# Scores behind each attend in a shared PSUM ring, fp32 scores for the first twelve pairs, and a planner that knows the shared port

## The chip, the cores and the metric

The kernel runs on one core of one Trainium2 chip. Its engines work side by side and meet through semaphores: PE (TensorE, matmuls; PEld is its weight load), ACT (ScalarE), DVE (VectorE), POOL (GpSimd), and SP, which issues all DMAs. SBUF holds tiles; PSUM, 8 banks of 2 KB for each of 128 partitions, takes what PE computes. The metric is the device time of one execution in microseconds, the median of several runs.

## The reference

Attention with a sigmoid in place of a softmax, then a gated product with a short convolution:

```python
scores = scale * np.matmul(q, k.transpose(0, 1, 3, 2)) - np.log(S)   # (8, 12, 448, 64)
attn = 1.0 / (1.0 + np.exp(-scores))
x = np.matmul(attn, v)                       # heads joined: (8, 448, 768)
gate_pre = sum over k of conv_w[k] * xp[:, k:k+S, :]     # 5 taps over time, per channel
gate = 1.0 / (1.0 + np.exp(-gate_pre))
out = (gate * (x @ w_val)) @ w_out
```

All inputs and the output are fp32.

## The kernel before

Two heads make a pair (128 channels on the partitions), so there are 8 x 6 = 48 pairs; six pairs are one batch. The first 12 pairs (FIRST_PAIRS) are batches 0 and 1; for them there are no products to run beside, or few.

**Precision.** Most matmuls work on values split into a high part in fp32r and a low remainder, three passes for one product (high x high, low x high, high x low). `split_qk` (L346) makes qk_hi by a cast on DVE or ACT and qk_lo by a subtraction on POOL (`sub`, L293), two of each for every pair. `scores` (L360, matmuls at L374) then multiplies keys and queries in three passes; the two heads use the two halves of the array's rows (64*128 tiles) at once. The keys beyond 3 x 128 of both heads form a fourth chunk, which uses all rows (`scores_rest`, L380, matmuls at L386).

**Attention.** `attention` (L390) applies the sigmoid on ACT. For the first 12 pairs it writes fp32 (a_single), and `attend` (L436) multiplies it with v in plain fp32. From pair 12 on the sigmoid stays in PSUM (L398), a scaled fp16 copy (L410, ACT) and its remainder (L411, DVE) go to the tile `a`, and v is scaled by a power of two and split into two fp16 parts as well (`v_scale`, L414). That power comes from the largest |v| (L443), spread over the partitions by a one-column matmul with ones at the end of an attend two pairs earlier (L464) into a spare column of ps_x, and worked out by one step on DVE (L421) and three on POOL (L423, L425, L427). In `attend`, L455 is the fourth chunk with all rows and columns, L461 the others, two heads in the two column halves (128*64 tiles).

**Gate and products.** `after` (L468) copies ps_x to x (L282 or L288), splits it into xs, and builds the gate from x by five taps (L290 or L288, then four of L508) and a sigmoid (L510). Batch 0 goes to a scratch in DRAM, and a seventh of it is loaded back behind each later batch's rows (L484, L501), so that a product has 448 + 64 = 512 columns. `product` (L515, matmuls at L529) is one block of 128 output channels: six parts of three matmuls, `val` from xs, then, gated at L541, `out` from g. There are 12 such products for each of seven batches.

**Weights.** `weight` (L320) loads 24 blocks as 64-bit words and turns each into fp32 on DVE (L313, L315, L329) and ACT (L317), then splits it (ACT and POOL).

**PSUM.** Before the change: two score tiles of two banks (ps_sc), one bank for the fourth chunk (ps_c3), one for attend's result (ps_x), two for products (ps_m).

**Order.** Nothing is in order of the source. Each step is put on record by `op` with the engines that may run it and their cost (`ways`), a due time (`prio`), and what it reads and writes. `tau(i)` is the due time of pair i: FIRST = 7.0 us a pair for the first 12, STEP after. `Plan.issue` (L137) then runs through time: each engine that is free takes the ready step with the smallest due time, and the steps are emitted in that order. A ring's tile may be taken again when all who used its last content are done. On the chip each engine's queue then runs strictly in this order. In the plan before, scores are groups of one chunk (first 12 pairs) or of two chunks (L580) with due times of their own, spread over a pair's time.

Of the kernel before, what the change touches and what calls it, by code (L numbers as in the profile page):

```python
# [23 lines left out]
P = 128  # L24
# [63 lines left out]
class Op:  # L88
    __slots__ = ("ways", "prio", "emit", "deps", "n", "start", "end", "eng", "after", "size")

    def __init__(self, n, ways, prio, emit, size):
        self.n, self.ways, self.prio, self.emit, self.size = n, ways, prio, emit, size
        self.deps, self.after = set(), None
        self.start = self.end = self.eng = None


class Plan:
# [39 lines left out]
    def issue(self):  # L137
# [12 lines left out]
        events, order, bus = [], [], 0.0  # L150
# [48 lines left out]
def attention_then_gate(  # L199
# [42 lines left out]
    a_ring = ring(sb, 5, [P, 2, 2 * S], F16, "a")  # L242
# [53 lines left out]
    FIRST, STEP = 7.0, 13.7  # L296
# [7 lines left out]
    def at_share(i, c):  # L304
        return ((0, 0.2, 0.5, 0.6) if i < FIRST_PAIRS else (0, 1 / 3, 2 / 3, 0.9))[c]


    def convert(w, t, prio, wide):
# [4 lines left out]
        op({"V": 0.6 * c}, prio, lambda e: nc.vector.tensor_scalar(  # L313
            low(), low().bitcast(U32), 2.0**-29, 7.0, op0=ALU.mult, op1=ALU.min), [], [t])
        op({"V": 0.8 * c}, prio + 0.1, lambda e: nc.vector.scalar_tensor_tensor(  # L315
            low(), high(), -0x80000000, low(), op0=ALU.bitwise_and, op1=ALU.bitwise_or), [], [t])
        op({"A": 0.55 * c}, prio + 0.2, lambda e: nc.scalar.activation(  # L317
            high().bitcast(F32), high().bitcast(F32), AF.Copy, scale=REBIAS), [], [t])

    def weight(n, j):  # L320
# [8 lines left out]
        op({"V": 0.7}, prio + 0.3, lambda e: nc.vector.scalar_tensor_tensor(  # L329
# [3 lines left out]
        op({"A": 0.51}, prio + 0.4, lambda e: copy(e, part(h), single().bitcast(F32)), [t], [h])  # L333
        op({"G": 1.2}, prio + 0.5, lambda e: sub(
# [11 lines left out]
    def split_qk(i):  # L346
# [3 lines left out]
        for n, cs in enumerate((slice(0, S), slice(S, QW))):  # L350
            op({"V": 0.4, "A": 0.58}, t - 11 + n, lambda e, cs=cs: copy(e, h()[:, cs], x()[:, cs]), [x], [h])
        for n, cs in enumerate((slice(0, S), slice(S, QW))):
            op({"G": 1.4}, t - 9 + n, lambda e, cs=cs: sub(
                e, l()[:, cs], x()[:, cs], h()[:, cs].bitcast(F32)), [x, h], [l])

    def terms(s):
        h, l = s["h"], s["l"]
        return (h, h), (l, h), (h, l)

    def scores(group):  # L360


        bufs, reads = [], []
        for i, c in group:
            b = st[i]["ps", c] = ps_sc.new()
            bufs.append(b)
            reads += [st[i]["h"], st[i]["l"]]

        def emit(e):
            for (i, c), b in zip(group, bufs):  # L370
                for n, (k, q) in enumerate(terms(st[i])):
                    for h, rows in enumerate(halves):
                        at = S + c * P
                        mm(b()[:, h, :S], k()[rows, at : at + P], q()[rows, :S],  # L374
                           start=(n == 0), stop=(n == 2))

        i, c = group[-1]
        op({"P": 0.4 + 0.585 * len(group)}, tau(i) + share(i, at_share(i, c)), emit, reads, bufs)

    def scores_rest(i):  # L380
        s = st[i]
        b = s["ps", 3] = ps_c3.new()

        def emit(e):
            for n, (k, q) in enumerate(terms(s)):
                mm(b()[:, :S], k()[:, QW - P :], q()[:, :S], start=(n == 0), stop=(n == 2))  # L386

        op({"P": 0.61}, tau(i) + share(i, at_share(i, 3)), emit, [s["h"], s["l"]], [b])

    def attention(i, c):  # L390

        s, t = st[i], tau(i) + share(i, at_share(i, c))
        b = s["ps", c]
        cost = 0.92 if c < 3 else 0.55
        p = (lambda: b()[:, :, :S]) if c < 3 else (lambda: b()[:, :S])
# [11 lines left out]
        a = s["a", c] = a_ring.new()
        part = lambda n: a()[:, :, n * S : (n + 1) * S] if c < 3 else a()[:, 0, n * S : (n + 1) * S]
        op({"A": cost}, t + 1, lambda e: sigmoid(p()), [], [b])
        op({"A": cost}, t + 2, lambda e: nc.scalar.activation(part(0), p(), AF.Copy, scale=A_SCALE), [b], [a])  # L410
# [240 lines left out]
```

## Time and profile before

| what | us |
|---|---|
| median of 3 runs | 674.22 |
| lowest, highest run | 672.52, 676.32 |
| the profiled execution | 673.52 |
| its span, first to last instruction | 671.7 |

A profile is one execution. Its page gives the busy time of each engine, the span in 40 slices, the chain of work that ended last, and the costliest groups of instructions; the trace behind it answers questions by window, tile or line. The ends of matmuls are modelled: the pace of PE is read from the starts. A row of the timeline has its start, its length, the engine, the line, what is written from what, the tile (rows*columns of the array for PE), and how many instructions are merged; in brackets stands idle time before it and what ended it. A row of a tile's view has the shortest, median and longest duration in ns; a row of waits has the total, the number of times and the longest.

### The profile page before, as it was taken

The page shows a single profiled execution, that of the slowest core. Times are in us where ns is not written, and L with a number is a line of the kernel's source. Part 1 is how long each engine was busy: PE and PEld are TensorE (multiplying, and loading weights), DVE is VectorE, ACT ScalarE, POOL GpSimd, SP SyncE. Part 2 cuts the span into 40 slices and gives each one's busy share as a digit, 9 for nine tenths or more (in the row PEclk, how much of TensorE's full clock was granted, in tenths as well). Part 3 has the DMA queues.
Part 4 walks back from the last instruction along what each step waited for, and adds up shares of the span by engine and source line. Part 5 has one row for each costly group of instructions (what it writes and reads, how often), then busy time and mean ns, then how long its engine had stood idle before and what let it go on. Part 6 is the DMA issues. An engine that isn't in the chain of part 4 may idle for free.

```text
span 671.7 us, 9920 instructions
## 1 busy us (share of the span) xinstructions
PE 645.9 (96%) x3540; PEld 441.7 (66%) x3540; DVE 511.3 (76%) x708; ACT 437.6 (65%) x671; POOL 311.0 (46%) x313
## 2 busy tenths in 40 slices
PE   7888889899999999999999999999999999999997
PEld 5433344577767777677776777767777677776786
DVE  4999999889759897598975989759897598864410
ACT  6777756667766677666776667766677666774111
POOL 4888766645334453344533445334453344520100
PEclk9899989799999999999999999999999999999999
DMA  7889542312333123321234212332123411011001
GB/s 284 273 278 299 171 149 60 111 51 70 102 96 85 52 70 102 109 71 52 71 101 116 65 52 70 101 110 72 52 71 102 121 58 52 25 49 44 1 33 62
DMA packets 49537, 65.66 MB, mean 98 GB/s; under 512 B 26448, under 2 KB 34128, under 8 KB 49488
## 3 DMA queue, kind: packets, MB, share of 16 engines
q1 hardware_dynamic: 49488, 65.03, 32.0%
q8 instruction: 28, 0.46, 0.3%
q14 instruction: 21, 0.17, 0.1%
HBM read 49.86 MB, written 15.15 MB: 97 GB/s over the span
## 4 chain that ended last, share of the span: by engine, by line
PE 81%; DVE 10%; DMA 3%; issue 3%; ACT 2%; POOL 1%; SPq 0%; DVEq 0%; POOLq 0%; ACTq 0%
PE ps_m L529 53%; PE ps_sc L374 11%; PE ps_x L461 10%; PE ps_x L455 3%; PE ps_c L386 3%; DVE gate L508 3%; DVE w_words L329 2%; DVE w_words L315 1%; DMA w_words<-w_val 1%; DVE w_words L313 1%; DMA first_x<-x 1%; DVE gate L290 1%; DVE qk_hi L284 1%; ACT a_single L398 1%; DMA xs<-first_xs 1%
## 5 line engine op out<-in xcount | busy, mean ns | idle before, releaser
L508 DVE SCALAR_TENSOR_TENSOR gate<-x,cw,gate 128x515 f32<-128x515 f32 (+3 forms) x168 | 167.6, 997 | 2.3
L529 PE MATMUL ps_m<-xs,w_val_hi 128*128 128x512 f32 x504 | 164.3, 407 | 3.1 <-DMA xs<-first_xs 2.6
L293 POOL TENSOR_TENSOR qk_lo<-qk_src,qk_hi 128x448 fp32r<-128x448 f32 x96 | 138.0, 1445 | 58.7 <-DVE qk_hi L284 29.4
L529 PE MATMUL ps_m<-g,w_out_hi 128*128 128x512 f32 x504 | 160.9, 400 | 0.0
L411 DVE SCALAR_TENSOR_TENSOR a<-ps_sc,a 128x896 f16<-128x896 f32 x108 | 115.0, 1078 | 1.2 <-ACT a L410 1.1
L529 PEld LDWEIGHTS ps_m<-xs,w_val_hi 128*128 128x128 f32 x504 | 92.8, 191 | 29.7 <-issue 6.9
L529 PEld LDWEIGHTS ps_m<-g,w_out_hi 128*128 128x128 f32 x504 | 92.4, 188 | 25.1 <-issue 4.0
L398 ACT ACTIVATE ps_sc<-ps_sc 128x896 f32<-128x896 f32 x108 | 93.1, 898 | 22.1 <-PE ps_sc L374 22.1
L529 PE MATMUL ps_m<-xs,w_val_lo 128*128 128x512 f32 x252 | 100.8, 400 | 0.0
L529 PE MATMUL ps_m<-g,w_out_lo 128*128 128x512 f32 x252 | 99.9, 397 | 0.0
L410 ACT ACTIVATE a<-ps_sc 128x896 f16<-128x896 f32 x108 | 96.7, 921 | 0.0
L293 POOL TENSOR_TENSOR xs<-x,xs 128x448 fp32r<-128x448 f32 x48 | 68.8, 1433 | 55.1 <-DVE xs L284 36.5
L374 PE MATMUL ps_sc<-qk_hi 64*128 64x448 f32 x288 | 62.9, 434 | 15.3 <-ACT a_single L398 14.5
L421 DVE TENSOR_SCALAR v_exp<-ps_x 128x1 int32<-128x1 int32 x36 | 5.7, 158 | 87.0 <-PE ps_x L464 55.5
L423 POOL TENSOR_SCALAR v_exp<-v_exp 128x1 int32<-128x1 int32 x36 | 10.6, 294 | 127.6 <-DVE v_exp L421 127.5
L293 POOL TENSOR_TENSOR g<-y,g 128x512 fp32r<-128x512 f32 x27 | 35.4, 1310 | 68.2 <-ACT g L282 58.5
L461 PE MATMUL ps_x<-a,v_hi 128*64 128x448 f16 x432 | 59.7, 357 | 0.0
L374 PEld LDWEIGHTS ps_sc<-qk_hi 64*128 64x128 f32 x288 | 27.2, 186 | 49.2 <-ACT a_single L398 20.4
L288 ACT ACTIVATE x<-ps_x,v_exp 128x448 f32<-128x448 f32 x36 | 23.0, 638 | 51.9 <-PE ps_x L464 40.6
L529 PEld LDWEIGHTS ps_m<-xs,w_val_lo 128*128 128x128 f32 x252 | 47.9, 190 | 11.7
L529 PEld LDWEIGHTS ps_m<-g,w_out_lo 128*128 128x128 f32 x252 | 47.3, 188 | 11.5
L374 PE MATMUL ps_sc<-qk_hi,qk_lo 64*128 64x448 f32 x288 | 53.2, 366 | 0.8 <-POOL qk_lo L293 0.8
(69 smaller groups left out, 959.3 us busy)
## 6 DMA issues: line engine op xcount, KB each, us to landing
qk_src<-qk SPq DMA_DIRECT2D x48, 480.0 KB, 3.6
v_src<-vs SPq DMA_DIRECT2D x48, 256.0 KB, 2.7
out_t<-y SPq DMA_DIRECT2D x42, 224.0 KB, 2.0
w_words<-w_val SPq DMA_DIRECT2D x12, 384.0 KB, 4.0
w_words<-w_out SPq DMA_DIRECT2D x12, 384.0 KB, 3.5
first_xs<-xs SPq DMA_DIRECT2D x6, 448.0 KB, 4.1
xs<-first_xs SPq DMA_DIRECT2D x42, 64.0 KB, 3.2
x<-first_x SPq DMA_DIRECT2D x42, 34.0 KB, 1.8
```

Of the source, the lines that this page charges most:

```text
L288: nc.scalar.activation(to, x, AF.Copy, scale=by)
L293: engines[eng].tensor_tensor(to, x, y, op=ALU.subtract)
L329: op({"V": 0.7}, prio + 0.3, lambda e: nc.vector.scalar_tensor_tensor(single(), single(), 3, t()[:, :, 0], op0=ALU.logical_shift_left, op1 ...
L374: mm(b()[:, h, :S], k()[rows, at : at + P], q()[rows, :S], start=(n == 0), stop=(n == 2))
L386: mm(b()[:, :S], k()[:, QW - P :], q()[:, :S], start=(n == 0), stop=(n == 2))
L398: nc.scalar.activation(to, p(), AF.Sigmoid, bias=-math.log(S), scale=1.0 / math.sqrt(D))
L410: op({"A": cost}, t + 2, lambda e: nc.scalar.activation(part(0), p(), AF.Copy, scale=A_SCALE), [b], [a])
L411: op({"V": 1.09 if c < 3 else 0.62}, t + 3, lambda e: nc.vector.scalar_tensor_tensor(part(1), p(), A_SCALE, part(0), op0=ALU.mult, op1=ALU ...
L455: mm(px()[:, :S], v()[:, :P], x(3)[:, 0, at : at + S], start=(n == 0), stop=False, skip_group_check=True)
L461: mm(px()[rows, :S], v()[:, o : o + D], x(c)[:, h, at : at + S], start=False, stop=(c == 2 and n == len(parts) - 1), skip_group_check=True)
L508: op({"V": 0.85}, t + 1 + j, lambda e, j=j: nc.vector.scalar_tensor_tensor(g()[:, j:], x()[:, : T + HALO - j], w(j), g()[:, j:], op0=ALU.m ...
L529: mm(po(), w()[:, c, :], x()[:, k, :], start=(c == 0 and j == 0), stop=(c == NC - 1 and j == 2))
```

## The change

- **Scores of the first 12 pairs in fp32.** They are not split any more: `terms` gives a single pass on the loaded qk tile itself.
- **One PSUM ring.** ps_sc, ps_c3 and ps_x become `ps_a`, three tiles of two banks, used in the order in which they are asked for. From pair 12 on that is: fourth chunk of pair i + 1, attend's result of pair i, chunks 0, 1, 2 of pair i + 1.
- **A chain on PE.** `attend` is two steps (the one-column matmul, the fourth chunk and chunks 0 and 1; then chunk 2), followed by the scores of the next pair (of the pair after the next among the first 12), chunks 0 and 1, then 2. Through the new field `then`, PE takes nothing else in between; the first step of an attend also waits until the sources of those scores are there.
- **The planner's port.** A step marked with port may run on DVE or POOL only while no other such step holds their shared port; YIELD lets a step with an earlier due time go first. Steps that read PSUM have port="". Costs are set anew, and more steps may run on either of two engines.
- **Other moves.** The steps that read PSUM get much earlier due times (t - 20, t - 30); the three steps for the power of two move from POOL to DVE; the load of first_xs moves from t + 2 to t - 6; tiles: a 5 to 3 and a_rest 2, g (and the weight words with it) 4 to 3, g2 2 to 3; STEP 13.7 to 13.6.

```diff
@@ Plan.issue
+                for _, n in ready[e]:
+                    o = self.ops[n]
+                    if held[e] not in (None, o):
+                        continue
+                    if e not in "VG" or e not in o.port:
+                        break
+                    x = "G" if e == "V" else "V"
+                    sooner = any(p < o.prio and x in self.ops[k].port for p, k in ready[x][:4])
+                    if port <= t and not (sooner and free[x] < t + self.YIELD):
+                        break
+                else:
                     continue
-                o = self.ops[heapq.heappop(q)[1]]
-                done.add(o.n)
+                for x in o.ways:
+                    ready[x].remove((o.prio, o.n))
+                held[e] = o.then
...
+                if e in "VG" and e in o.port:
+                    port = t + cost
@@ tiles
-    a_ring = ring(sb, 5, [P, 2, 2 * S], F16, "a")
+    a_ring = ring(sb, 3, [P, 2, 2 * S], F16, "a")
+    rest_ring = ring(sb, 2, [P, 1, 2 * S], F16, "a_rest")
...
-    g_ring = ring(sb, 4, [P, 2, T], F32R, "g")
-    g2_ring = ring(sb, 2, [P, 2, T], F32R, "g2")
+    g_ring = ring(sb, 3, [P, 2, T], F32R, "g")
+    g2_ring = ring(sb, 3, [P, 2, T], F32R, "g2")
...
-    ps_sc = ring(ps, 2, [P, 2, 512], F32, "ps_sc")
-    ps_c3 = ring(ps, 1, [P, 512], F32, "ps_c3")
-    ps_x = ring(ps, 1, [P, 512], F32, "ps_x")
+    ps_a = ring(ps, 3, [P, 2, 512], F32, "ps_a")
@@ scores
+    def terms(i):
+        if i < FIRST_PAIRS:
+            return ((st[i]["qk"],) * 2,)
+        h, l = st[i]["h"], st[i]["l"]
         return (h, h), (l, h), (h, l)
...
+        return op({"P": cost}, tau(i) + 0.1 * cs[0], emit, sources(i), bufs)
@@ v_scale
-        op({"G": 0.4}, t + 0.2, lambda _: nc.gpsimd.tensor_scalar(
+        op({"V": 0.12}, t + 0.2, lambda _: nc.vector.tensor_scalar(
...
@@ attend
+        first = op({"P": 2.5 if single else 2.0}, t, lambda e: (rest(e), chunks((0, 1))),
+                   [a[0], a[1], a[3], *values] + ([ones, m] if m else []), [px])
+        first.then = op({"P": 0.76 if single else 0.56}, t, lambda e: chunks((2,)), [a[2], *values], [px])
+        return first
@@ after
-            out_of_ps = {"A": 0.64}, t, lambda e: scaled(e, own(), px()[:, :S], v()[:, 3:4].bitcast(F32)), [px, v]
+            out_of_ps = {"A": 0.64}, t - 20, lambda e: scaled(e, own(), px()[:, 0, :S], v()[:, 3:4].bitcast(F32)), [px, v]
...
+        if f:
+            op({"S": 0.1}, t - 6, lambda e: nc.sync.dma_start(
+                xs()[:, :, S:].bitcast(F32), first_xs[c]()[:, :, n : n + SL]), [first_xs[c]], [xs], P * 1024)
@@ the main order
+    for i in range(FIRST_PAIRS, NPAIRS):
+        split_qk(i)
+
+    def score(i, after=None):
+        first = scores(i, (0, 1))
+        first.then = scores(i, (2,))
+        if after:
+            after.then.then = first
+            after.deps.update(d for b in sources(i) for d in b.writers)
+        for c in range(3):
+            attention(i, c)
+
+    def rest(i):
+        scores_rest(i)
+        attention(i, 3)
+
+    for i in range(2):
+        score(i)
+        rest(i)
     for i in range(NPAIRS):
         for n, j in blocks[2 * i : 2 * i + 2]:
             weight(n, j)
+        if FIRST_PAIRS <= i + 1 < NPAIRS:
+            rest(i + 1)
+        o = attend(i)
         after(i)
-        if i + 2 < NPAIRS and i + 2 >= FIRST_PAIRS:
+        if FIRST_PAIRS <= i + 2 < NPAIRS:
             v_scale(i + 2)
+        if i + 2 < FIRST_PAIRS:
+            score(i + 2, o)
+            rest(i + 2)
+        elif FIRST_PAIRS <= i + 1 < NPAIRS:
+            score(i + 1, o)
```

More of the change, by code (lines that the diff above doesn't have):

```diff
@@ L1 @@
+import bisect
 import heapq
@@ L88, with __init__ @@
 class Op:
[L89 to L93, printed above, removed]
+    __slots__ = ("ways", "prio", "emit", "deps", "n", "start", "end", "eng", "after", "size", "port", "then")
+    def __init__(self, n, ways, prio, emit, size, port):
+        self.n, self.ways, self.prio, self.emit, self.size, self.port = n, ways, prio, emit, size, port
+        self.deps, self.after, self.then = set(), None, None
         self.start = self.end = self.eng = None
@@ L149, in issue @@
         ready = {e: [] for e in engines}
-        events, order, bus = [], [], 0.0
+        held = dict.fromkeys(engines)
+        events, order, bus, port = [], [], 0.0, 0.0
         def release(o, t):
@@ L400, in attention @@
         if i < FIRST_PAIRS:
-            r, tag = (g2_ring, "g2") if c == 0 else (a_ring, "a")
-            a = r.new(lambda: sb.tile([P, 2, S], F32, name="a_single", tag=tag, bufs=r.n))
+            r, tag = (rest_ring, "a_rest") if c == 3 else (g2_ring, "g2") if (c + i) % 2 else (a_ring, "a")
+            a = r.new(lambda: sb.tile([P, 1 if c == 3 else 2, S], F32, name="a_single", tag=tag, bufs=r.n))
             s["a", c] = a
-            to = (lambda: a()) if c < 3 else (lambda: a()[:, 0])
-            op({"A": cost}, t + 1, lambda e: sigmoid(to()), [b], [a])
+            op({"A": cost}, t, lambda e: sigmoid(a()), [b], [a])
             return
[L407 to L410, printed above, removed]
-        op({"V": 1.09 if c < 3 else 0.62}, t + 3, lambda e: nc.vector.scalar_tensor_tensor(
-            part(1), p(), A_SCALE, part(0), op0=ALU.mult, op1=ALU.subtract), [b], [a])
+        a = s["a", c] = (a_ring if c < 3 else rest_ring).new()
+        part = lambda n: a()[:, :, n * S : (n + 1) * S]
+        op({"A": cost}, t, lambda e: sigmoid(p()), [], [b])
+        op({"A": cost}, t + 0.4, lambda e: scaled(e, part(0), p(), A_SCALE), [b], [a], port="")
+        op({"V": 1.09 if c < 3 else 0.62}, t + 0.5, lambda e: nc.vector.scalar_tensor_tensor(
+            part(1), p(), A_SCALE, part(0), op0=ALU.mult, op1=ALU.subtract), [b], [a], port="")
     def v_scale(i):
@@ L436, in attend @@
     def attend(i):
-        s, t = st[i], tau(i + 1) + share(i + 1, 0.37)
-        px = s["px"] = ps_x.new()
+        s, t = st[i], tau(i + 1) + share(i + 1, 0) - 0.5
+        px = s["px"] = ps_a.new()
         a = [s["a", c] for c in range(4)]
@@ L450, in attend, with rest, chunks @@
             ]
-        reads = a + ([s["v"]] if i < FIRST_PAIRS else [s["vh"], s["vl"]])
-        def emit(e):
+        single = i < FIRST_PAIRS
+        values = [s["v"]] if single else [s["vh"], s["vl"]]
+        def rest(e):
+            if m:
+                mm(px()[:, 1, :1], ones(), m(), start=True, stop=True)
             for n, (v, x, at) in enumerate(parts):
-                mm(px()[:, :S], v()[:, :P], x(3)[:, 0, at : at + S], start=(n == 0), stop=False,
+                mm(px()[:, 0, :S], v()[:, :P], x(3)[:, 0, at : at + S], start=(n == 0), stop=False,
                    skip_group_check=True)
-            for c in range(3):
+        def chunks(cs):
+            for c in cs:
                 for n, (v, x, at) in enumerate(parts):
@@ L521, in product @@
             if n == "val":
-                x, reads = s["xs"], s["xh"] + s["xl"]
+                x, reads = s["xs"], s["xs_in"]
             else:
@@ L535, in product @@
         if n == "val":
-            g, gate = (g2_ring if m % 3 == 2 else g_ring).new(), st[b * NP + m]["g"]
+            g, gate = (g2_ring if m % 2 else g_ring).new(), st[b * NP + m]["g"]
             gv[b, m] = g
@@ L559, in attention_then_gate @@
     nc.vector.memset(ones(), 1.0)
-    busy = ps.tile([P, 512], F32, name="ps_c3", bufs=1)
+    busy = ps.tile([P, 512], F32, name="ps_m", bufs=2)
     for _ in range(WARM):
```

135 lines of the change are left out of this document (53 added, 82 removed).

## The prediction

> **What bounds the kernel now.** Three views, in this order: the page for shares and clock, the busy times by window for where TensorE waits, the chain and the timeline for what a pair costs.
>
> ```profile
> PE 645.9 (96%) x3540; PEld 441.7 (66%) x3540; DVE 511.3 (76%) x708; ACT 437.6 (65%) x671; POOL 311.0 (46%) x313
> PEclk9899989799999999999999999999999999999999
> PE 81%; DVE 10%; DMA 3%; issue 3%; ACT 2%; POOL 1%; SPq 0%; DVEq 0%; POOLq 0%; ACTq 0%
> ```
>
> ```profile
> 0.00:60.00 60.00, 49.74 (x295) 26.16 (x297) 49.32 (x62) 42.97 (x75) 44.47 (x45) 0.97 0.85 279
> 60.00:121.50 61.50, 50.04 (x247) 24.16 (x245) 60.14 (x73) 43.42 (x73) 43.54 (x36) 0.96 0.50 157
> 121.50:137.00 15.50, 15.50 (x72) 10.94 (x73) 12.88 (x22) 9.27 (x16) 8.45 (x9) 0.83 0.19 57
> 137.00:617.00 480.00, 480.00 (x2705) 341.13 (x2703) 377.52 (x534) 332.22 (x494) 210.29 (x222) 1.00 0.27 76
> ```
>
> The columns are the stretch, then busy us of PE, PEld, DVE, ACT and POOL, the granted clock, the DMA share and GB/s. From 137 to 617 PE has no idle time at all. Everything else is before: up to 121.5 PE idles 60 + 61.5 - 49.74 - 50.04 = 21.7 us, and the clock of 0.97, 0.96 and 0.83 costs at most 1.8 + 2.5 + 2.6 = 6.9 us of full speed. I count 5, as part of those stretches is idle anyway. So there are two questions: how much PE work does the change remove, and how much of the early 26.7 us.
>
> What a steady pair costs, from the chain that ended last:
>
> ```profile
> 212.89 1.82 PE ps_x L461 x18
> ...
> 296.83 1.82 PE ps_x L461 x18
> ...
> 625.64 42.26 PE ps_m L529 x180
> ```
>
> Six attends lie between the first two rows: 83.94 / 6 = 13.99 us a pair. The last row is 60 product parts of three matmuls: less 0.16 of final drain, 42.1 / 60 = 0.70 each. Twelve parts to a pair are 8.40, so scores, attend and the switches between them take 5.59.
>
> ```profile
> 402.74 0.36 PE L374 MATMUL ps_sc<-qk_lo,qk_hi 64*128 64x448 f32 x2
> 403.04 0.73 PE L529 MATMUL ps_m<-xs,w_val_hi 128*128 128x512 f32 x2
> ...
> 408.75 0.55 PE L455 MATMUL ps_x<-a,v_hi 128*128 128x448 f16 x2
> ...
> 409.42 0.57 PE L461 MATMUL ps_x<-a,v_hi 128*64 128x448 f16 x4
> ...
> 410.96 0.36 PE L461 MATMUL ps_x<-a,v_lo 128*64 128x448 f16 x2
> 411.25 0.18 PE L464 MATMUL ps_x<-vm,ones 128*128 128x1 bf16 x1
> 411.36 0.47 PE L374 MATMUL ps_sc<-qk_hi 64*128 64x448 f32 x2
> 411.67 0.36 PE L374 MATMUL ps_sc<-qk_hi,qk_lo 64*128 64x448 f32 x2
> 411.87 0.37 PE L374 MATMUL ps_sc<-qk_lo,qk_hi 64*128 64x448 f32 x2
> ```
>
> Starts tell the pace, the ends are modelled. A score pass takes 411.87 - 411.67 = 0.20. Where the tile shape changes a step is 0.10 longer: 402.74 to 403.04 is 0.30, 411.36 to 411.67 is 0.31, 410.96 to 411.25 is 0.29 where a pass is 0.19.
>
> **The change part by part: the steady pairs.** Three chunks now run in one group behind attend, where 1.5 groups of two stood. New sum per pair: 0.67 for L455 with its switch (408.75 to 409.42), 1.73 for the 18 L461 (409.42 to 410.96 and a pass), 0.10 to leave their shape, 0.11 on the first score, 9 x 0.203 = 1.83 for scores, 0.20 back to products, 0.61 for the rest chunk between products (three passes), and 0.08 for the one-column matmul, which moves ahead of L455 where no shape changes (it takes 0.11 now): 5.33. That is 0.26 less; by how the switches merge I bound it at 0.15 and 0.45. Over 36 pairs **-9.4 us** (-5 to -16).
>
> What it adds is a wait. In the ring of three the order is rest, attend's ps_x, chunk 0, 1, 2, so chunk 2 takes the slot of the ps_x that attend has just left, and needs it read by the scaled copy on ACT and the exponent read on DVE. All products queue behind it on PE.
>
> ```profile
> L421 DVE TENSOR_SCALAR v_exp<-ps_x x36: 145/158/160, 106.6 to 593.3; 128x1 int32<-128x1 int32 x36
> L288 ACT ACTIVATE x<-ps_x,v_exp x36: 634/636/647, 130.9 to 619.7; 128x448 f32<-128x448 f32 x36
> L398 ACT ACTIVATE ps_sc<-ps_sc x108: 863/899/935, 110.4 to 609.6; 128x896 f32<-128x896 f32 x108
> L508 DVE SCALAR_TENSOR_TENSOR gate<-x,cw,gate x168: 734/754/1772, 72.4 to 624.0; 128x515 f32<-128x515 f32 x42, 128x514 f32<-128x514 f32 x42, 128x513 f32<-128x513 f32 x42, 128x512 f32<-128x512 f32 x42
> ```
>
> The last pass of attend starts at s and ends at s + 0.36 (row 410.96); the copy takes 0.64, so the slot is free at s + 1.05. PE reaches chunk 2 at s + 0.19 + 0.21 + 6 x 0.20 = s + 1.6. The slack is 0.55. A sigmoid of 0.90 begun just before makes it 0.35 late, a blocked gate step of 1.77 with the 0.16 behind it up to 1.3. ACT is busy 332 of 480 us and both reads get first priority, so I take 0.05 a pair: **+1.8 us** (0 to +20).
>
> The three one-column exponent steps go from POOL to DVE, at most 3 x 0.16 a pair; DVE has 480 - 377.5 idle in the steady stretch, which hides 17 us. With that cover gone the scaled values, and so the next attend, would come as much later. Without cover the smaller score buffers would cost too; here each is refilled only after the attend that read it.
>
> **The first twelve pairs.**
>
> ```profile
> 13.51 1.02 PE L455 MATMUL ps_x<-a_single,v_src 128*128 128x448 f32 x2 [0.43 <-ACT a_single L398]
> 14.46 2.48 PE L461 MATMUL ps_x<-a_single,v_src 128*64 128x448 f32 x12
> 16.87 0.47 PE L374 MATMUL ps_sc<-qk_hi 64*128 64x448 f32 x2
> ```
>
> ```profile
> 41.96 0.47 PE L374 MATMUL ps_sc<-qk_hi 64*128 64x448 f32 x2
> ...
> 42.76 0.47 PE L386 MATMUL ps_c<-qk_hi 128*128 128x448 f32 x1
> ...
> 43.57 0.47 PE L374 MATMUL ps_sc<-qk_hi 64*128 64x448 f32 x2
> ...
> 63.04 1.02 PE L455 MATMUL ps_x<-a_single,v_src 128*128 128x448 f32 x2
> ...
> 112.29 0.91 PE L455 MATMUL ps_x<-a_single,v_src 128*128 128x448 f32 x2
> ```
>
> An attend takes 3.36 (13.51 to 16.87), a chunk alone 0.80, a rest chunk 0.81: 6.6 us a pair. The fp32 attend gives the price of an fp32 matmul: 12 records in 2.41 us, run in pairs, so 0.40 a record and, at two records, 0.80 a matmul. Three fp32 chunks in one group are 2.6 with the switches, the rest 0.84, with attend 6.8 a pair: 12 x 0.23 = **+2.8 us** (0 if a chunk costs 0.75, +5 if it costs 0.95 as L455 does). No row shows fp32 in the scores' 64-row tiles. The Trainium skill, FP8 and Floating Point Precision (TensorE Precision Notes), says that true fp32 takes four passes through the array, where the old form made three. By it a chunk would cost 4 x 0.20 = 0.81 and the sum would not move.
>
> PE could thus do a pair in 6.8, but attends 0, 6 and 11 start at 13.51, 63.04 and 112.29: 8.25 a pair, then 9.85. What holds them?
>
> ```profile
> PEld ps_sc L374 <- ACT a_single L398: 20.4, 15, 2.6
> PE ps_sc L374 <- ACT a_single L398: 14.5, 11, 2.1
> ```
>
> ```profile
> L293 POOL TENSOR_TENSOR qk_lo<-qk_src,qk_hi x96: 1141/1392/1838, 4.7 to 587.7; 128x448 fp32r<-128x448 f32 x48, 128x512 fp32r<-128x512 f32 x48
> L284 DVE CAST qk_hi<-qk_src x53: 377/416/1389, 14.0 to 583.0; 128x448 fp32r<-128x448 f32 x36, 128x512 fp32r<-128x512 f32 x17
> ```
>
> PE waits for sigmoids; ACT's queue holds them behind weight steps, which wait for DVE, and DVE's casts stretch from 0.38 to 1.39 while POOL subtracts. DVE is busy 60 of 61.5 us. The change takes 24 subtractions of 1.39 (33 us) and as many casts from this stage, and attention here no longer needs DVE or POOL at all. Next in line is the DMA:
>
> ```profile
> qk_src<-qk SPq DMA_DIRECT2D x48, 480.0 KB, 3.6
> v_src<-vs SPq DMA_DIRECT2D x48, 256.0 KB, 2.7
> ...
> w_words<-w_val SPq DMA_DIRECT2D x12, 384.0 KB, 4.0
> ...
> first_xs<-xs SPq DMA_DIRECT2D x6, 448.0 KB, 4.1
> ...
> first_x<-x SPq DMA_DIRECT2D x6, 226.0 KB, 4.2
> ```
>
> A pair of the first six with two weight blocks moves 2178 KB, 2.23 MB; at the 279 GB/s of the first window, 8.0 us. So the first six gain little, and the next five can fall from 9.85 towards 6.8. The source tile of qk is now held until the scores have read it, and attend waits for the next pair's: about one pair's time for a load that lands in 3.6. Weight words have three buffers for four; deferred weights hide that, and without that the 0.8 us of pace is lost again. Idle time afterwards: 1.1 at the start, 0.8 to the first attend, 6 x (8.0 - 6.8) = 7.2, 3 for the last five and the passage to products (the first_xs slice is loaded earlier, so products wait for it less), 2 for the clock: 14.1, against 26.7: **-12.6 us** (-21 with 6 left, 0 with nothing gained). The port model in the planner only reorders; I give it no term of its own, its effect is in this one.
>
> Sum: -9.4 + 1.8 + 2.8 - 12.6 = -17.4. The profiled execution took 673.52, its span 671.7, so 1.8 lies around it: 654.3 + 1.8 = **656 us**. The median shown is 674.22, 0.7 above that execution; I leave that out.
>
> **The rivals.**
> Loads bind throughout: attend waits for the next qk, the early idle time stays. For: 279 GB/s already. Against: 157 GB/s after 60. 671.7 - 9.4 + 1.8 + 2.8 + 1.8 = 669 us.
> Better than forecast: DMA does not bind, 6 us idle stay (-8), and switches save 0.45 (-7): 641 us.
> The halves of an fp32 score do not run side by side: 12 x 3 x 0.80 = +28.8, of which 7 fall into idle time: 656 + 28.8 - 7.4 = 677 us. Against: fp32 in column halves does run in pairs.
> Slower: chunk 2 waits for ps_x in every pair. Another 0.53 us a pair eats the whole gain (19.2 / 36). At 1.0 a pair it is 656 + 36 x 0.95 = 690 us. For: the 1.77 step; against: the slack of 0.55. The Trainium skill, TensorE: Matmul & The Clock Gate (A second HAM failure mode), reports that cycling through PSUM with small pauses made the clock gate drop and recover again and again. This trace has a clock of 1.00 where PE never pauses and drops it only in the stage with pauses, which agrees. If each pair's pause also brought one drop like the first window's (1.8 us lost), that would be 36 x 1.8 = 65 us more, 755; I give it 0.01 of the 0.08.
>
> **How the numbers follow.** Forecast 0.60 (645 to 667), loads bind 0.15, better 0.10, fp32 halves 0.07, slower 0.08. The range 637 to 672 leaves out the last two and the edges. About 0.5% is what a measurement here tells from no change: faster means under 670.9. Faster: 0.58 + 0.10 + 0.10 = 0.78; same 0.10; slower 0.12.
>
> **What would show it.** Attends 13.7 apart, all of a pair's scores behind them; attend 11 starting near 100; no POOL subtraction of qk before that; PE's waits in the steady stretch under 2 us. A wait of PE for the copy of ps_x in each pair, or attends still 8 to 10 apart at 60 to 110 us, would make it wrong.

## The result and the profile after

The changed kernel takes 644.1 us (median of 4 runs, 643.12 to 646.61) against 674.85 (672.52 to 676.32) for the kernel before on the same chip. The ratio is 0.9553, with a 95% interval of 0.9514 to 0.9593: about 30 us faster. The forecast was 656 us, in a range of 637 to 672: the right sign and inside the range, but 0.9 below its main part (645 to 667), with a gain of 18 forecast where there were 30. The profiled execution took 644.21 us with a span of 642.4, where the one before had 671.7: 29.3 us to account for.

From the page after, the busy times with their shares, and the granted clock in 40 slices:

```profile
PE 631.1 (98%) x3456; PEld 436.2 (68%) x3456; DVE 480.6 (75%) x889; ACT 421.8 (66%) x646; POOL 136.8 (21%) x109
PEclk9999999999999999999999999999999999999999
```

PE's busy time fell by 14.8 us (645.9 to 631.1), and its idle time, span less busy, by 14.5 (25.8 to 11.3). POOL lost more than half of its work (311.0 to 136.8), and DVE, which took some of it over, has less too (511.3 to 480.6). The clock no longer drops in any slice.

The busy times by window after (stretch, then PE, PEld, DVE, ACT, POOL, granted clock, DMA share, GB/s):

```profile
0.00:60.00 60.00, 56.17 (x266) 24.30 (x268) 39.11 (x86) 39.81 (x63) 3.78 (x13) 1.00 0.84 287
60.00:100.00 40.00, 37.94 (x164) 16.75 (x160) 34.85 (x66) 28.09 (x49) 7.56 (x6) 1.00 0.65 206
100.00:121.50 21.50, 20.04 (x114) 13.97 (x111) 21.50 (x39) 18.02 (x28) 6.57 (x5) 1.00 0.29 87
137.00:600.00 463.00, 462.87 (x2657) 339.89 (x2654) 364.07 (x665) 317.67 (x478) 111.09 (x80) 1.00 0.26 77
```

Up to 121.5 us PE now idles 3.83 + 2.06 + 1.46 = 7.35 us, where it idled 21.7, and the clock that cost up to 6.9 there and just behind costs nothing. In the first 60 us POOL is busy 3.78 us instead of 44.47, the DVE 39.11 instead of 49.32. From 137 on PE is full as it was: what is gained there is less work, not less waiting.

The chain that ended last, with its steady attends (the 18 passes of L478, L461 before):

```profile
242.53 1.82 PE ps_a L478 x18
...
324.49 1.82 PE ps_a L478 x18
```

Six pairs apart: 81.96 / 6 = 13.66 us a pair, where it was 13.99. The timeline after shows where the 0.33 went; each row is one step with its start, and the starts give the pace:

```profile
405.68 0.18 PE L468 MATMUL ps_a<-vm,ones 128*128 128x1 bf16 x1
...
405.72 0.54 PE L470 MATMUL ps_a<-a_rest,v_hi 128*128 128x448 f16 x2
...
406.38 0.57 PE L478 MATMUL ps_a<-a,v_hi 128*64 128x448 f16 x4
...
407.92 0.36 PE L478 MATMUL ps_a<-a,v_lo 128*64 128x448 f16 x2
...
408.20 0.47 PE L387 MATMUL ps_a<-qk_hi 64*128 64x448 f32 x2
...
408.31 0.64 ACT L302 ACTIVATE x<-ps_a,v_exp 128x448 f32<-128x448 f32 x1 [2.50 <-PE ps_a L478]
...
408.51 0.37 PE L387 MATMUL ps_a<-qk_hi,qk_lo 64*128 64x448 f32 x2
...
408.98 0.16 DVE L433 TENSOR_SCALAR v_exp<-ps_a 128x1 int32<-128x1 int32 x1 [3.09 <-ACT x L302]
...
409.53 0.36 PE L387 MATMUL ps_a<-qk_hi 64*128 64x448 f32 x2
...
410.23 0.73 PE L547 MATMUL ps_m<-g,w_out_hi 128*128 128x512 f32 x2
...
410.80 0.40 PE L547 MATMUL ps_m<-g,w_out_lo 128*128 128x512 f32 x1
```

The one-column matmul takes 0.04 (405.68 to 405.72), the fourth chunk 0.66, the 18 passes 1.82, and the scores run without a break from 408.20. The tile shape changes once from attend to the scores. The two reads of attend's result (L302 on ACT, L433 on DVE) show the slack of the new wait: chunk 2 starts at 409.53, and the exponent read, which starts only when the copy has ended, is done at 408.98 + 0.16 = 409.14.

The first stage on PE, from the timeline after:

```profile
1.08 6.17 PE L581 MATMUL ps_m<-ones 128*128 128x128 bf16 x60 [1.08 <-DVE ones L577]
7.19 2.53 PE L387 MATMUL ps_a<-qk_src 64*128 64x448 f32 x12
...
32.28 2.53 PE L387 MATMUL ps_a<-qk_src 64*128 64x448 f32 x12
34.74 1.02 PE L398 MATMUL ps_a<-qk_src 128*128 128x448 f32 x2
35.59 0.92 PE L470 MATMUL ps_a<-a_single,v_src 128*128 128x448 f32 x2
36.44 2.48 PE L478 MATMUL ps_a<-a_single,v_src 128*64 128x448 f32 x12
38.84 2.53 PE L387 MATMUL ps_a<-qk_src 64*128 64x448 f32 x12
41.30 1.02 PE L398 MATMUL ps_a<-qk_src 128*128 128x448 f32 x2
...
57.55 1.02 PE L470 MATMUL ps_a<-a_single,v_src 128*128 128x448 f32 x2 [0.22 <-ACT a_single L411]
```

Where nothing waits, a pair takes 41.30 - 34.74 = 6.56 us, and its three fp32 chunks 34.74 - 32.28 = 2.46, 0.82 each. Attend 0 starts at 13.90 and attend 6 at 57.55, 7.28 apart (8.25 before); attend 11 starts at 97.09 (112.29 before). From attend 6 to attend 11 a pair takes 7.91, with 2.07 us of idle time in all; 27 product matmuls (L547) stand in that stretch, as many as in the like stretch before.

### The profile page after: what moved, and what is told of

Same layout as the page of the kernel before. It is cut to its first block, busy times and chain, and to the rows that moved or that the text cites. A ratio compares the mean times of both kernels' runs of the same rounds, so it can differ in the third digit from the quotient of the medians.

```text
span 642.4 us, 9603 instructions
## 1 busy us (share of the span) xinstructions
PE 631.1 (98%) x3456; PEld 436.2 (68%) x3456; DVE 480.6 (75%) x889; ACT 421.8 (66%) x646; POOL 136.8 (21%) x109
## 4 chain that ended last, share of the span: by engine, by line
PE 86%; DVE 7%; DMA 4%; ACT 1%; issue 1%; POOL 0%; ACTq 0%; DVEq 0%
PE ps_m L547 54%; PE ps_a L387 12%; PE ps_a L478 12%; PE ps_a L470 4%; PE ps_a L398 4%; DMA w_words<-w_val 3%; DVE gate L526 2%; PE ps_m L581 1%; DMA w_words<-w_out 1%; DVE w_words L340 1%; DVE a L423 1%; ACT a_single L411 1%; DVE w_words L326 1%; DVE w_val_lo L307 0%; DVE w_words L324 0%
## 5 line engine op out<-in xcount | busy, mean ns | idle before, releaser
L307 POOL TENSOR_TENSOR qk_lo<-qk_src,qk_hi 128x448 fp32r<-128x448 f32 x72 | 102.5, 1438 | 296.9 <-ACT qk_hi L296 296.9
L547 PE MATMUL ps_m<-xs,w_val_hi 128*128 128x512 f32 x504 | 161.6, 401 | 2.7 <-ACT xs L296 1.1
L547 PE MATMUL ps_m<-g,w_out_hi 128*128 128x512 f32 x504 | 159.6, 397 | 0.0
L526 DVE SCALAR_TENSOR_TENSOR gate<-x,cw,gate 128x515 f32<-128x515 f32 (+3 forms) x168 | 136.6, 813 | 0.2
L411 ACT ACTIVATE ps_a<-ps_a 128x896 f32<-128x896 f32 (+1 forms) x144 | 113.7, 806 | 21.6 <-PE ps_a L398 21.4
L547 PEld LDWEIGHTS ps_m<-xs,w_val_hi 128*128 128x128 f32 x504 | 93.0, 188 | 31.8 <-issue 6.4
L423 DVE SCALAR_TENSOR_TENSOR a<-ps_a,a 128x896 f16<-128x896 f32 x108 | 114.1, 1084 | 0.2 <-ACT a L302 0.2
L547 PEld LDWEIGHTS ps_m<-g,w_out_hi 128*128 128x128 f32 x504 | 93.2, 188 | 26.2 <-issue 5.6
L547 PE MATMUL ps_m<-g,w_out_lo 128*128 128x512 f32 x252 | 100.3, 398 | 0.0
L547 PE MATMUL ps_m<-xs,w_val_lo 128*128 128x512 f32 x252 | 100.3, 398 | 0.0
L302 ACT ACTIVATE a<-ps_a 128x896 f16<-128x896 f32 x108 | 95.3, 920 | 0.1
L302 ACT ACTIVATE x<-ps_a,v_exp 128x448 f32<-128x448 f32 x36 | 22.9, 635 | 58.2 <-PE ps_a L478 58.2
L478 PE MATMUL ps_a<-a,v_hi 128*64 128x448 f16 x432 | 59.7, 357 | 0.0
L296 ACT CAST g<-y 128x512 fp32r<-128x512 f32 x40 | 24.7, 617 | 49.6 <-DVE y L559 49.6
L547 PEld LDWEIGHTS ps_m<-g,w_out_lo 128*128 128x128 f32 x252 | 47.4, 188 | 11.1
L547 PEld LDWEIGHTS ps_m<-xs,w_val_lo 128*128 128x128 f32 x252 | 47.4, 188 | 11.0
L433 DVE TENSOR_SCALAR v_exp<-ps_a 128x1 int32<-128x1 int32 x36 | 5.7, 157 | 58.8 <-ACT x L302 57.9
L559 DVE TENSOR_TENSOR y<-ps_m,gate 128x448 f32<-128x448 f32 x84 | 31.7, 419 | 21.8 <-PE ps_m L547 21.6
L387 PE MATMUL ps_a<-qk_hi 64*128 64x448 f32 x216 | 43.5, 400 | 0.7 <-DVE v_exp L433 0.6
L296 ACT CAST qk_hi<-qk_src 128x512 fp32r<-128x512 f32 (+1 forms) x71 | 42.3, 600 | 1.2 <-DMA qk_src<-qk 1.0
```

The source lines that it names most:

```text
L296: nc.scalar.copy(to, x)
L302: nc.scalar.activation(to, x, AF.Copy, scale=by)
L307: engines[eng].tensor_tensor(to, x, y, op=ALU.subtract)
L387: mm(b()[:, h, :S], k()[rows, at : at + P], q()[rows, :S], start=(n == 0), stop=(n == len(terms(i)) - 1))
L411: nc.scalar.activation(to, p(), AF.Sigmoid, bias=-math.log(S), scale=1.0 / math.sqrt(D))
L423: op({"V": 1.09 if c < 3 else 0.62}, t + 0.5, lambda e: nc.vector.scalar_tensor_tensor(part(1), p(), A_SCALE, part(0), op0=ALU.mult, op1=A ...
```

## Experiments

Each time is a median beside runs of the kernel before on the same chip; ratios are to that kernel. The runs came from more than one chip, so small differences between kernels of different groups are read from ratios.

**fp32 scores alone, in the kernel before.** The scores of the first twelve pairs read the loaded tile in one pass; the rest stays as before.

```diff
+        if "h" not in s:
+            return ((s["qk"],) * 2,)
         h, l = s["h"], s["l"]
...
-    for i in range(NPAIRS):
+    for i in range(FIRST_PAIRS, NPAIRS):
         split_qk(i)
```

> The kernel before with one part of the change alone: scores of the first 12 pairs in fp32 from the loaded tile, no splits for them. Theory A: most of the early gain is there, idle time of PE before the steady pairs falls from 21.7 us to 8 to 14, the steady pair stays at 13.99, 654 to 664 us. Theory B: DVE is still stretched by the other subtractions, 666 us or more.

Measured 659.86 us, ratio 0.9781 (0.9749 to 0.9813): 14.3 us, half of the change's gain. Its windows:

```profile
0.00:60.00 60.00, 56.14 (x256) 21.94 (x258) 31.70 (x55) 42.42 (x73) 22.62 (x30) 0.97 0.85 279
60.00:100.00 40.00, 40.00 (x167) 15.81 (x164) 37.09 (x54) 29.26 (x49) 21.10 (x19) 1.00 0.65 208
100.00:121.50 21.50, 18.51 (x101) 11.38 (x100) 21.26 (x33) 14.96 (x23) 12.96 (x14) 1.00 0.34 103
```

PE idles 3.86 + 0 + 2.99 = 6.85 us to 121.5, no more than in the changed kernel. A steady pair stays at 14.01 (84.03 us for six). So the whole gain in early idle time is had by fp32 alone; the clock still drops once, 0.97 in the first window.

**The change with split scores throughout.**

```diff
     def terms(i):
-        if i < FIRST_PAIRS:
+        if i < 0:
             return ((st[i]["qk"],) * 2,)
...
-    for i in range(FIRST_PAIRS, NPAIRS):
+    for i in range(NPAIRS):
         split_qk(i)
```

> The changed kernel with split scores for the first 12 pairs too (24 casts and 24 subtractions more before the steady pairs, three fp32r passes a chunk). Theory A: the port and DVE bind again, attends 0 to 11 are 8 to 9.5 us apart, 655 to 668 us. Theory B: the planner places the splits without loss, and PE has 12 x 0.6 us less to do, so 640 to 648 us.

Measured 663.72 us, 0.9841 (0.9812 to 0.9871). One row for the whole early stretch:

```profile
0.00:121.50 121.50, 99.43 (x540) 56.10 (x541) 92.68 (x170) 87.01 (x147) 40.15 (x40) 0.95 0.66 219
```

PE idles 22.07 us there, as before the change (21.7), while a steady pair takes 13.66. The two runs are mirror images: fp32 earns the early time and nothing later, the rest of the change the steady time and nothing early. On top of that rest fp32 is worth 663.72 - 644.1 = 19.6 us, alone 14.3; so some 5 us come only with both together, and no run divides these.

**PE not held.** The chain from attend to the scores is broken up: PE takes the step that is due first.

```diff
-                held[e] = o.then
+                held[e] = None
```

> The changed kernel with a planner that does not hold PE between attend and the scores (held[e] = None); due times alone order them. If the steady gain of 0.33 us a pair comes from fewer changes of tile shape, it shrinks by 0.10 to 0.20 us for each shape change that comes back: the steady pair at 13.75 to 14.1 and 648 to 660 us. If it comes from the ring alone, 643 to 646 us.

Measured 665.64 us, 0.987 (0.984 to 0.9899), 21.5 us above the changed kernel and more than expected. A steady pair takes 14.05 (84.31 us for six): 36 x 0.39 = 14.0 of the 21.5. PE has no idle time in that stretch, so the 0.39 are work. From its timeline:

```profile
351.79 0.35 PE L478 MATMUL ps_a<-a,v_lo 128*64 128x448 f16 x2
352.08 0.73 PE L547 MATMUL ps_m<-g,w_out_hi 128*128 128x512 f32 x2
352.64 0.40 PE L547 MATMUL ps_m<-g,w_out_lo 128*128 128x512 f32 x1
352.97 0.57 PE L478 MATMUL ps_a<-a,v_hi 128*64 128x448 f16 x4
```

In this pair a product part stands between attend's chunks 1 and 2. It takes 0.89 from start to start where 0.70 is its pace among its like, and the step ahead of it 0.29 instead of 0.19: two switches more, some 0.3. The rest of the 21.5 is lost earlier; the granted clock from 100 to 121.5 is 0.86.

**The port model.** The planner's steps on DVE and POOL no longer exclude each other.

```diff
-size=0, port="VG"):
+size=0, port=""):
```

> The changed kernel with a planner that no longer knows the port (every step port=""); ring, chain, fp32 scores, costs and due times stay. If the early gain comes from attention no longer needing DVE and POOL (theory A), the first attends stay 7.2 to 7.8 us apart and the time is 643 to 650 us. If it comes from the planner's knowledge of the port (theory B), DVE steps are stretched behind POOL again, attends go back to 8 us or more apart, and the time is 655 us or more.

Measured 676.33 us, 1.0029 (1.0009 to 1.0048): the whole gain is gone. The theory that the rest of the change stays fast without the model fell. From the windows and the groups by line:

```profile
137.00:600.00 463.00, 447.75 (x2540) 319.54 (x2539) 406.03 (x662) 298.97 (x429) 151.40 (x112) 1.00 0.26 76
```

```profile
L547 PE MATMUL ps_m<-xs,w_val_hi 128*128 128x512 f32 x504 | 162.6, 403 | 10.1 <-DVE y L559 9.3 <-POOL xs L307 0.8
```

PE idles 15.25 us in the steady stretch, with products waiting for the gated y of DVE; DVE is busy 406 us instead of 364, and a steady pair takes 14.40. But the step costs in the changed planner are those of an engine undisturbed. Without the model they may simply be too short, and DVE's queue planned too full. Two further runs part this.

**Average costs, no model, subtractions on POOL.** The longer costs of before are put back (eight in all, three are shown), and the subtractions for weights and xs run on POOL alone as before.

```diff
-size=0, port="VG"):
+size=0, port=""):
...
-        op({"V": 0.36 * c}
+        op({"V": 0.6 * c}
...
-        op({"G": 1.02, "V": 0.56}, prio
+        op({"G": 1.2}, prio
...
-        op({"G": 1.15, "V": 0.62}, t + 1
+        op({"G": 1.3}, t + 1
```

> The changed kernel without the port model (port="" everywhere) and with the longer DVE and POOL costs of before for casts of weights, subtractions and gate steps, subtractions of weights, qk and xs on POOL alone. The run without the port model but with the new costs took 676. If the port model itself is needed (theory B), this one is slow too: 665 us or more. If the new costs are merely too short for a planner that does not know the port, honest averages repair it: 645 to 658 us, about what fp32 scores alone (660) and the steady gain of 12 us leave, and the steady pair is back at 13.7.

**The model kept, subtractions on POOL.**

```diff
-        op({"G": 1.02, "V": 0.56}, prio
+        op({"G": 1.02}, prio
...
-        op({"G": 1.15, "V": 0.62}, t + 1
+        op({"G": 1.15}, t + 1
```

> The changed kernel in which the subtractions of weights and xs may run on POOL alone again (72 of them), as before the change; the port model stays. If what matters in the port model is that work can leave POOL for DVE, where a subtraction of 448 columns took 0.62 us against 1.4, the early stage is port-bound again: attend 11 starts at 102 or later and the time is 650 to 662 us. If it is the order alone, 643 to 648 us.

Measured 659.94 us, 0.9773 (0.9751 to 0.9796), and 655.74 us, 0.9737 (0.9703 to 0.9771). Both have those subtractions on POOL; what is between them, 0.0036 of 674 or about 2.4 us, is the model with its costs against the longer averages, and the intervals overlap. From the second to the changed kernel it is 0.0184, about 12 us: DVE doing 67 of these subtractions in 0.55 to 0.62 us each (medians) where POOL in the second run takes 1.03 to 1.26. The first run falls between its two expectations: a steady pair takes 13.88 there without idle time of PE (462.13 us busy of 463), where the second run is back at 13.66 from 400 on. So the two differ in the steady stretch by 0.22 us a pair, which the second loses again elsewhere. The second run missed its expectation in place: the first six attends are 6.97 apart and attend 11 is at 96.14, no later than in the changed kernel; the loss is elsewhere (PE idles 3.86 us from 60 to 100 at a clock of 0.94, 4.00 from 100 to 137 at 0.92, and 3.69 from 137 to 400).

**The scaled copy of attend's result three times.** The copy on ACT that frees the PSUM slot for chunk 2 is repeated; the output is the same.

```diff
-            out_of_ps = {"A": 0.64}, t - 20, lambda e: scaled(e, own(), px()[:, 0, :S], v()[:, 3:4].bitcast(F32)), [px, v]
+            out_of_ps = {"A": 1.9}, t - 20, lambda e: [scaled(e, own(), px()[:, 0, :S], v()[:, 3:4].bitcast(F32)) for _ in range(3)], [px, v]
```

> The changed kernel with the scaled copy of attend's result made three times into the same place (from pair 12 on), 1.27 us more before the tile is free. By the prediction's slack of 0.55 us PE then waits 0.5 to 0.9 us for chunk 2 in every pair: the steady pair at 14.2 to 14.5 and 662 to 676 us. If the ring's order has more slack than that, or chunk 2 does not hang on the copy, the steady pair stays at 13.7 and the time below 650.

Measured 696.27 us, 1.0326 (1.0305 to 1.0348): more than expected. Its timeline:

```profile
410.30 0.47 PE L387 MATMUL ps_a<-qk_hi 64*128 64x448 f32 x2
...
410.41 1.97 ACT L302 ACTIVATE x<-ps_a,v_exp 128x448 f32<-128x448 f32 x3 [0.99 <-PE ps_a L478]
...
412.41 0.16 DVE L433 TENSOR_SCALAR v_exp<-ps_a 128x1 int32<-128x1 int32 x1 [2.94 <-ACT x L302]
...
412.63 0.47 PE L387 MATMUL ps_a<-qk_hi 64*128 64x448 f32 x2 [0.84 <-DVE v_exp L433]
...
418.27 0.44 PE L398 MATMUL ps_a<-qk_hi 128*128 128x448 f32 x1 [0.38 <-DVE a L423]
```

Chunk 2 starts 2.33 us behind chunk 0 (410.30 to 412.63), where it was 1.33 (408.20 to 409.53): 1.00 later, for copies that take 1.33 longer. So the slack was 0.33 us. PE waits a second time, 0.38, at the next fourth chunk: the sigmoid of chunk 0 and what follows it have slipped, and the ring gives that chunk's slot out next. A steady pair takes 91.67 / 6 = 15.28, 1.62 more. This is the slower rival, brought about on purpose: its mechanism is real, and the second wait, which the rival did not have, makes it dearer.

**The reads of attend's result planned late.**

```diff
-        op({"V": 0.16}, t - 30, lambda
+        op({"V": 0.16}, t + 4, lambda
...
-            out_of_ps = {"A": 0.64}, t - 20,
+            out_of_ps = {"A": 0.64}, t + 4,
```

> The changed kernel with the two steps that read attend's result (scaled copy on ACT, exponent on DVE, from pair 12 on) given late due times (t + 4 for t - 20 and t - 30), so that other ready steps go first. If chunk 2 of the scores hangs on them as the prediction says, with a slack of about 0.5 us, PE waits for them in many pairs: 0.3 to 1.5 us a pair, 655 to 700 us. If the ring's order leaves more slack than that, 643 to 647 us.

Measured 652.51 us, 0.9699 (0.9675 to 0.9723), with no stall in the steady stretch (PE busy 463.00 of 463) and 13.69 a pair: a miss. Most of the 8 us are lost between 100 and 137 (7.5 idle, clock 0.86). The due time hardly changes when the reads run once the order has settled (the copy starts 0.40 us behind the start of attend's last matmul, the median of the steady pairs, as in the changed kernel), so this run says nothing of the slack; the one with three copies does. Every sixth pair shows something else, the exponent read ahead of the copy:

```profile
404.72 0.16 DVE L433 TENSOR_SCALAR v_exp<-ps_a 128x1 int32<-128x1 int32 x1 [1.36 <-PE ps_a L478]
404.91 0.64 ACT L302 ACTIVATE x<-ps_a,v_exp 128x448 f32<-128x448 f32 x1 [0.33 <-DVE v_exp L433]
```

Here the copy waits for the exponent read, 404.72 + 0.16 = 404.88.

**An extra load in the early pairs.** 256 KB more are copied in DRAM for each of the pairs 2 to 7; nobody reads them.

```diff
+        if 2 <= i < 8:
+            z = scratch([P, VW], F32, f"extra{i}")
+            op({"S": 0.1}, t - 12, lambda e: nc.sync.dma_start(z(), vs[i]), [], [z], P * VW * 4)
```

> The changed kernel with one more transfer of 256 KB a pair for pairs 2 to 7 (v copied to a place in DRAM that nobody reads), 0.85 us a pair at 309 GB/s. If the DMA binds the first pairs at 7.28 us (the prediction's term, with its rate put right), attends 0 to 6 go to 7.8 to 8.2 us apart and the time to 647 to 651 us. If PE and ACT bind them, they stay at 7.0 to 7.4 and the time at 643 to 646.

Measured 647.17 us, 0.9596 (0.9572 to 0.9619), some 3 us more than the change, though the intervals overlap. Attends 0 to 6 are 7.44 apart, which neither expectation has. The loss is not spread over the pairs. From its chain and its timeline:

```profile
14.46 5.69 DMA w_words<-w_val
22.58 1.02 PE ps_a L401 x2
```

```profile
21.17 0.58 ACT L302 ACTIVATE w_words<-w_words 128x384 f32<-128x384 f32 x1 [3.35 <-DVE w_words L326]
21.63 1.71 ACT L414 ACTIVATE a_single<-ps_a 128x896 f32<-128x896 f32 x2
```

One wait of 2.96 us at 22.58: the sigmoids stand on ACT behind a weight step, whose load is late. The attends behind it, at 23.43, 31.70, 38.40, 45.02, 51.73 and 58.48, are then 6.6 to 6.8 apart but for the first, near PE's own 6.56, with the DMA share at 0.93 and 309 GB/s from 13.84 to 58.48. The first, 8.27, holds a drop of the clock behind the pause (0.86 from 20 to 25 and 0.80 from 25 to 30). That rate is the changed kernel's own, so only some 0.3 MB more were moved there: the run shows what a late load costs (one stop), not where the limit of the DMA is.

**The loads of w_out 42 us later.** In the due time of these blocks, 42 + 3.5 * j becomes 84 + 3.5 * j.

> The changed kernel with the due times of the second matrix's weight blocks 42 us later (84 for 42), which takes some 2 MB out of the first seven pairs. If the DMA binds the first six pairs at 7.28 us (309 GB/s), they go to 6.6 to 6.9 us apart, near PE's own 6.56, and attend 6 starts 2 to 4 us earlier. If ACT or DVE bind them, they stay at 7.2 to 7.4. The total 641 to 648 us either way.

Measured 651.65 us, 0.9677 (0.9659 to 0.9695). That is above the 641 to 648 expected either way. The order of the loads before 50 us did not change, so this didn't touch the stage that it was meant for: that attend 6 starts at 55.07, in the place expected of a DMA limit, says nothing of one. PE idles 3.88 from 60 to 100 and 3.82 from 100 to 137; why it loses there is open.

**Fewer warm-up matmuls:** 36, and 12, in place of 60.

```diff
-WARM = 60
+WARM = 36
```

> The changed kernel with 36 warm-up matmuls for 60. They end at 7.2 us in the changed kernel, and the first scores wait for nothing else. If PE bounds from the first score on, the end moves by up to 2.4 us: 641.5 to 643.5. If the loads bound the first pairs, or the clock drops after a shorter warm-up, 644 to 647 us.

> The changed kernel with 12 warm-up matmuls for 60; 36 brought 2.1 us, and the first scores began at 4.7. With 12 they can begin once qk has landed, near 4. If the clock is granted as before, 640.5 to 642.5 us; if it starts low without the warm-up, the first scores take twice as long and the time is 642 to 646 us.

Measured 642.08 us, 0.9544 (0.9525 to 0.9564), and 643.43 us, 0.9538 (0.9521 to 0.9555). By ratio to the kernel before neither can be told from the change's 0.9553; the spans of the profiled executions are 640.0 and 641.3 against 642.4. The start of the run with 12:

```profile
1.08 1.46 PE L581 MATMUL ps_m<-ones 128*128 128x128 bf16 x12 [1.08 <-DVE ones L577]
4.06 4.85 PE L387 MATMUL ps_a<-qk_src 64*128 64x448 f32 x12 [1.51 <-DMA qk_src<-qk]
8.84 1.36 PE L398 MATMUL ps_a<-qk_src 128*128 128x448 f32 x2
10.13 2.53 PE L387 MATMUL ps_a<-qk_src 64*128 64x448 f32 x12
```

Its first scores start when qk has landed, at 4.06, but run at half pace (4.85 for what takes 2.53 next), so attend 0 starts at 13.44, hardly before the 13.90 of the change. With 36 the first scores start at 4.71 at full pace, attend 0 at 12.29 and attend 6 at 55.15, 2.40 earlier than in the change. So the loads did not hold attend 6 where it was.

## Why the prediction was right, and where it was off

It named the two places where time could be had, early idle time and the shapes in a steady pair, and both paid. Step by step, against the span:

| step of the prediction | forecast | measured |
|---|---|---|
| steady pair | 13.73 us (-9.4 in all) | 13.66 (-11.9) |
| wait of chunk 2 for attend's result | +1.8 | one wait of 0.6, part of the idle time below |
| fp32 in the first pairs, 6.6 to 6.8 a pair | +2.8 | 6.56 a pair, about 0 |
| early idle time and clock, 26.7 to 14.1 | -12.6 | 7.35, clock 1.00: about -19.4 |
| warm-up | none | +1.33 (4.84 to 6.17), by chance of the run |

The measured column, with 21.7 idle and 5 of clock taken for before, adds up to -30.0, where the spans give -29.3; the 5 is an estimate. Every term of the forecast erred to the same side, so nothing cancelled but the warm-up, which is luck: the same 60 matmuls take 4.80 to 6.31 us in the runs that have them.

**The steady pair** was worked out rightly. Leaving attend's shape costs 0.10 (407.92 to 408.20 holds a pass of 0.19), entering the scores' another 0.10 (408.20 to 408.51 is 0.31), as the sum had it. The scores take 2.03 from first start to the next product, and the first two product matmuls take 0.57 (410.23 to 410.80) where two of a part's three take 0.47; 2.03 + 0.10 = 2.13, and the sum had 2.14. What is left of the 0.07 is the one-column matmul, 0.04 instead of 0.08, and about 0.01 each in attend's fourth chunk (0.66 for 0.67), its 18 passes (1.82 for 1.83) and elsewhere. The run without the hold shows that it is the chain that brings it.

**The wait** was priced about right, for a wrong reason. The forecast had both reads of attend's result side by side and a slack of 0.55; the exponent read starts where the copy ends, and the slack is 0.33, as the run with three copies measured it. The trace before showed that already: L421 at 412.13 names ACT's x as its releaser, and the copy, begun at 411.46, had ended at 412.10. Still no blocked gate step or sigmoid came in between but once, by the view of the waits after (total, times, longest):

```profile
PE ps_a L387 <- DVE v_exp L433: 0.6, 1, 0.6
```

It is not that the exponent read needs the copy. In the kernel before, 18 of the 36 pairs have the exponent read first and the copy behind it, and the run with late reads has five such pairs. In all runs these two reads, where one is on ACT and the other on DVE, follow one another, in either order, the second at least 0.03 us behind the end of the first. Whether the chip or the program's semaphores keep them apart isn't settled.

**fp32 scores**: the halves of the array do run side by side, at 0.82 a chunk, nearly the same as three split passes (0.80). The Trainium skill, FP8 and Floating Point Precision (TensorE Precision Notes), has four passes for fp32; by that 4 x 0.203 is 0.81, and the trace agrees. The +2.8 was too much: three chunks take 2.46 for 2.6, and an attend 38.84 - 35.59 = 3.25 for 3.36.

**The early idle time** is the step that was mis-sized, and its error, 6.8 with the clock, is over half of the 12 us. The term "6 x (8.0 - 6.8) = 7.2" took the 279 GB/s of the window before for what the DMA can do. That was a mean with slack in it: shorter stretches, of before and of after, show more.

```profile
5.00:10.00 5.00, 4.20 (x38) 2.75 (x35) 1.93 (x3) 2.15 (x5) 4.54 (x4) 1.00 0.98 381
```

```profile
30.00:35.00 5.00, 5.00 (x25) 1.99 (x26) 4.76 (x11) 3.57 (x7) 0.10 (x1) 1.00 1.04 369
```

The like stretch after, from attend 0 to attend 6:

```profile
13.90:57.55 43.65, 40.90 (x169) 14.63 (x168) 33.96 (x72) 30.94 (x51) 3.45 (x7) 1.00 0.91 309
```

309 GB/s, 7.28 a pair, and 43.65 - 40.90 = 2.75 us of idle time in place of 7.2. The run with the extra load shows that the term was wrong in kind too: loads cost no even toll on every pair but one stop where one came late, through a weight step in ACT's queue, and the pairs behind it ran near PE's pace. The changed kernel has the same stop, smaller: its longest pause in this stretch, 1.30 us at 22.02, stands behind a weight step on ACT (at 20.61, after 1.30 of waiting), whose weight words were loaded by 19.48. The second mis-sized piece is the clock: 2 us were kept for it, but it never dropped before the end. With a pause of 2.96 in place of the 1.30, the clock of the first window is 0.97 again.

Two signs that the prediction named came out otherwise. Attends still 8 to 10 apart at 60 to 110 us were to make it wrong, and they are 7.91 apart, not near 6.8. That is not waiting: the pace of 6.8 left out the nine product parts that lie between these attends, some 6.3 us at 0.70 each, and PE idles only 2.07 there. And POOL's first subtraction of qk comes at 84.2, ahead of attend 11, as the split of pair 12 needs it.

**No term of its own for the planner** was half right. Against the longer averages the port model brings a few us at most by these runs, and the intervals overlap. But the freedom that came with it, subtractions on DVE where POOL took about twice as long, is worth about 12 us, which the forecast didn't price; the run without it loses this from 60 to 137 us and in the steady stretch. And the new costs need the model: with them alone, the run without it is no faster than the kernel before. What the model brings to the kernel before by itself wasn't tried.

**The rivals.** Loads did not bind throughout, as that rival had it, but they are not out of the way: of the chain that ends with the scores at 62 us after, 24.5 us are loads of weight words, and what a fourth buffer for these would bring wasn't tried. The fp32 halves ran side by side; chunk 2 waits in no steady pair as the kernel stands, though a copy 0.33 us longer would bring that rival up. The one that came nearest is "better than forecast" at 641 us: 7.35 us of idle time left where it had 6, and 0.33 a pair where it had 0.45.

## What to carry to other kernels

A rate that a trace shows is a lower bound of what the DMA can do, not its limit: before it enters a sum as a limit, look at shorter stretches (279 GB/s over 60 us hid 381 over five), and whether anything waited for a load. Parts of a change that act in different stages (here fp32 early, the chain in the steady pairs) are best priced and tried apart, each in the kernel that lacks the other. A planner's costs and its model of what engines share belong together: costs of undisturbed engines without the model cost here as much as the whole change brings.

## What the runs showed that was not expected

- The 60 warm-up matmuls took 6.17 us, where they took 4.84 in the kernel before; 36 took 3.69 (to 4.71, when the scores start). It isn't the change: the changed kernel without the hold and the one with the late loads of w_out took 4.80 and 4.96 for the same 60, and fp32 scores alone in the kernel before 5.29.
- With 12 warm-up matmuls PE ran at half pace up to about 9 us, while the granted clock of that window reads 1.00: at the start the clock row doesn't show it, the spacing of starts does.
- In the run with three copies PE pauses twice in every steady pair, 0.84 and 0.38 us, and the clock stays at 1.00. The Trainium skill, TensorE: Matmul & The Clock Gate (A second HAM failure mode), tells of a clock that drops again and again when PE cycles through PSUM with small pauses; in this run it did not.
- POOL's work goes with a stretch of more of DVE's steps than the casts which the forecast named. The second of the three DVE steps that build a weight block, by the view of its line (shortest, median and longest in ns), after:

```profile
L326 DVE SCALAR_TENSOR_TENSOR w_words<-w_words x24: 543/556/1257, 10.2 to 100.3; 128x384 int32<-128x384 int32 x24
```

and the same step before, at over twice the median:

```profile
L315 DVE SCALAR_TENSOR_TENSOR w_words<-w_words x24: 544/1258/1626, 8.4 to 106.1; 128x384 int32<-128x384 int32 x24
```

Before, the 20 of them that ran beside a POOL step have a median of 1.36 us, and the other four took 0.56 at most; after, 21 ran beside none and took 0.58 at most.
